# One core: v stores from the ScalarE queue to SP one unit later, z stores in half the issues, squares from GpSimd to ScalarE

## The chip, the cores and the metric

The kernel runs on one core of a Trainium2 chip. The metric is the device time of one execution in microseconds. Five engines work side by side, each with its own queue in order: TensorE (PE, with its weight loads PEld), VectorE (DVE), ScalarE (ACT), GpSimd (POOL) and SyncE (SP), which only issues DMAs. Time before the change: 1584.96 us, median of three runs (1580.27 to 1590.88).

## The reference

The input x has 8 batches of 3072 rows and 256 columns. Three things follow each other:

```
X = rfft(x, axis=1);  Y = soft(X @ (w_r + i w_i) + bias);  y = irfft(Y)        # soft: shrink by 0.01, real and imaginary
h = max(y @ w_in, 0);  g = (s * h^2 + b) @ w_out                               # 256 -> 2048 -> 256
logits = g @ w_gate;  e = argmax(logits)                                       # 8 experts
out[t] = p(t) * (max(g[t] @ w1[e], 0) @ w2[e])  for the first 768 tokens of each expert, 0 for the others
```

## The kernel before

The transform along 3072 = 48 x 64 rows is done as matrix products in stages, with the intermediate results in device memory. For a batch b: `f1_mm` (eight steps) multiplies x by the 48-point matrix, ScalarE copies the result to `z` and four DMAs store it to `zd`. Then twelve *groups* p: `g_load` loads a pair `zp`; `g_a` multiplies it by the second transform matrix (PE `pf`, L278; ScalarE copy `l`, L281); `g_b` and `g_b2` mix the channels with the weights (PE `pmx`, L355) and add the bias on VectorE (L364, L375 to L378); `g_soft` clips and subtracts on VectorE (`cl` L349, `t` L350); `g_c` multiplies by the inverse matrix (PE `pi`, L393), ScalarE copies to `v` (L395) and the ScalarE queue issues the store to `vd` (L397). Eight *inverse steps* follow: `i2_load` loads `u` from `vd` (L403), `i2_mm` multiplies it (PE `pi`, L419), ScalarE casts the result to `ah` (L422), GpSimd squares `ah` into `asq` (L425, bf16), and VectorE transposes the same PSUM tile into `at` (L434), which is stored to `ad` (L439).

The dense layer works on `ah` in *units*: `s_unit` has four products of 384 columns into one PSUM tile `ph` (L757), ScalarE's relu `r` (L762) and VectorE's square `qb` (L763). Eight units are one i, 64 units a batch, 512 units the kernel. A tile `ph`, the forward step's `pz` and the inverse step's `pi` share two PSUM buffers (tag `h`); the tile of an inverse step is free when both the cast and the transposes have read it. After eight units `lg_set` turns the squares and `asq` into logits (bounds that tell which tokens are certainly of one expert), `lg_out` copies them (L793) and `lg_fin` reduces them (L804). Tokens that the bounds leave open go into a list (GpSimd indirect DMAs, L911) and are computed exactly in the tail; batch 1 also holds four *exact blocks* (`x_steps`), whose squared rows `xq` are stored to `sd`.

The order of the work around the units is written by a planner in `run`: each unit k has a list of steps with ranks (loads 0, groups 1, second loads 2, logits 3, forward steps 4, inverse steps 5, zero stores of `out` 6, L1978). The groups of batch b + 1 run beside the units of batch b, from unit 64b - GROUP_LEAD on, a new group every five units, with the steps of a group 0, 2, 4, 4.1 and 8 units after its start; `g_load` is put six units ahead. Batch 1's groups have a schedule of their own (from unit 26, one every two units). The inverse steps and the forward steps of batch b + 2 are put where a cost is least: the load of a unit, 3 more if the unit already has such a step, 1 more for each neighbour that has one, and what the next unit lacks to 1.5. A step may put stores into the list `later`; they are issued in the next unit, right after `s_unit`, before that unit's other steps:

```
self.s_unit(b, i, u)
while self.later:
    self.later.pop(0)()
for e in sorted(plan.pop(64 * b + k, []), key=lambda e: e[:3]):
    e[3]()
```

Before the change the z and `at` stores go by `later` to SP; the v stores, the squares and the exact blocks' stores are issued at once.

Of the kernel before, what the change touches and what calls it, by code (L numbers as in the profile page):

```python
# [14 lines left out]
AF = mybir.ActivationFunctionType  # L15
ALU = mybir.AluOpType
# [3 lines left out]
C = 256  # L20
# [3 lines left out]
M1 = 48  # L24
# [7 lines left out]
TD = 256  # L32
# [92 lines left out]
S_FROM, S_TO = 19, 62  # L125
LIST_AT = 60
XP = 3
INV_LOAD_AT = 54
FIRST_GROUPS_AT = 26
GROUP_LEAD = 9  # L130
GROUP_CYCLE = 5
GROUP_STEPS = (("g_a", 0), ("g_b", 2), ("g_b2", 4), ("g_soft", 4.1), ("g_c", 8))
FIRST_STEPS = (("g_a", 0.3), ("g_b", 1.3), ("g_b2", 2), ("g_soft", 2.6), ("g_c", 5))
# [17 lines left out]
class Kern:  # L151
# [54 lines left out]
    def f1_load(self, b, c):  # L206

        xv = self.I["x"][b].rearrange("(a n) c -> a n c", n=M2)
        if b == 0 and c % 2 == 1:
            xs = [self.stage()[:, 0:2 * C].rearrange("p (n c) -> p n c", n=2) for k in range(2)]  # L210
            for k in range(2):
                for r in range(2):
                    n2 = 8 * c + 4 * r + 2 * k
                    self.nc.sync.dma_start(out=xs[k][64 * r:64 * r + M1], in_=xv[:, n2:n2 + 2, :])
        else:
            pool, tag = (self.mo, "u") if b == 0 and c > 3 else (self.wk, "x")
            xp = pool.tile([128, 4, C], F32, tag=tag, name="x", bufs=4 if tag == "x" else 3)
            for r in range(2):
                n2 = 8 * c + 4 * r
                self.nc.sync.dma_start(out=xp[64 * r:64 * r + M1], in_=xv[:, n2:n2 + 4, :])  # L220
            xs = [xp[:, 0:2], xp[:, 2:4]]
        self.xt[b, c] = xs

    def f1_mm(self, b, c):

        nc = self.nc
        xs = self.xt.pop((b, c))
        if b or c % 2 == 1:
            ph = self.hp.tile([128, 2, 512], F32, tag="h", name="pz")
            ps = [ph[:, 0], ph[:, 1]]  # L230
        else:
            ps = [self.psum("pz") for r in range(2)]
        for k in range(2):
            for r in range(2):
                h = slice(64 * r, 64 * r + M1)
                nc.tensor.matmul(ps[r][64 * k:64 * k + 64, :], self.f1[h], xs[k][h].rearrange("p a c -> p (a c)"),  # L236
                                 start=True, stop=True, skip_group_check=True)
        if b:
            zz = self.wk.tile([128, 2, 2, C], F32, tag="z", name="z", bufs=2)
            nc.scalar.copy(out=zz.rearrange("p r a c -> p r (a c)"), in_=ph)  # L240

            def store():
                for r in range(2):
                    for k in range(2):
                        n2 = 8 * c + 4 * r + 2 * k
                        nc.sync.dma_start(out=self.zs[b][n2:n2 + 2].rearrange("n q c -> q n c"), in_=zz[64 * k:64 * k + M1, r])
            self.later.append(store)
            return
        for r in range(2):
            t = 2 * c + r  # L250
            k = t % 11
            pool, tag, n = ((self.wk, "v", 3), (self.wk, "t", 3), (self.mo, "ah", 2), (self.mo, "asq", 2),
                            (self.wk, "zp", 3))[min(k // 2, 4)]
            z = pool.tile([128, 2, C], F32, tag=tag, name="z", bufs=n)
            if r == 1:
                nc.vector.tensor_copy(out=z.rearrange("p a c -> p (a c)"), in_=ps[r])
            else:
                nc.scalar.copy(out=z.rearrange("p a c -> p (a c)"), in_=ps[r])
            for k in range(2):
                n2 = 8 * c + 4 * r + 2 * k  # L260
                nc.sync.dma_start(out=self.zs[b][n2:n2 + 2].rearrange("n q c -> q n c"), in_=z[64 * k:64 * k + M1])
# [126 lines left out]
    def g_c(self, b, p):  # L388
        nc = self.nc
        t = self.Y.pop((b, p))  # L390
        ps = self.psum("pi1")
        for gi in range(2):
            nc.tensor.matmul(ps[:, gi * C:(gi + 1) * C], self.e[:, 2 * p + gi], t[:, gi * C:(gi + 1) * C], start=True, stop=True)  # L393
        v = self.wk.tile([128, 512], F32, tag="v", name="v", bufs=3)
        nc.scalar.copy(out=v, in_=ps)  # L395
        dst = self.vd[b].rearrange("n (r g) c -> (n r) (g c)", r=4)
        nc.scalar.dma_start(out=dst[:, 2 * p * C:(2 * p + 2) * C], in_=v)  # L397


    def i2_load(self, b, i):  # L400
# [6 lines left out]
    def i2_mm(self, b, i):  # L407

        nc = self.nc
        u = self.u.pop((b, i))  # L410
        ah = self.aT[b, i] = self.mo.tile([128, 2, TC], F32R, tag="ah", name="ah", bufs=2)
        ps = self.hp.tile([128, 2, 512], F32, tag="h", name="pi2")
        for h in range(2):
            for n in range(4):
                for r in range(2):
                    o = ps[:, r, 4 * M1 * h:4 * M1 * (h + 1)].rearrange("p (m n) -> p m n", n=4)
                    p = slice(64 * r, 64 * r + M1)
                    for k in range(2):
                        nc.tensor.matmul(o[64 * k:64 * k + 64, :, n], u[p, n, 128 * k + h:128 * k + 128:2], self.f1t[p],  # L419
                                         start=True, stop=True, skip_group_check=True)  # L420
        pv = ps[:, :, :TC].rearrange("p r (m n) -> p m r n", n=4)
        nc.scalar.copy(out=ah.rearrange("p h (m r n) -> p (h m) r n", r=2, n=4), in_=pv)  # L422
        af = ah.bitcast(F32)
        self.asq[b, i] = self.mo.tile([128, 2, TC], BF16, tag="asq", name="asq", bufs=2)
        nc.gpsimd.tensor_tensor(out=self.asq[b, i], in0=af, in1=af, op=ALU.mult)  # L425
        self.at[b, i] = pv

    def i2_rows(self, b, i):
# [21 lines left out]
    def f1_items(self, b):  # L450
        it = []
        for k in range(8):
            def f(k=k):
                self.f1_mm(b, k)
                if b:
                    self.x_ahead(8 * b + k + (XP if b < 3 else XP - 1))
            it.append(f)
        return it

    def x_ahead(self, n):  # L460

        while self.xn <= min(n, 8 * self.B - 1):
            self.f1_load(*divmod(self.xn, 8))
            self.xn += 1
# [535 lines left out]
    def x_steps(self, dtile, lgpool, ga, out, m0, hidden, rows, ptile, keep=None, yout=None):  # L1000

        nc = self.nc
# [7 lines left out]
                x["y"] = ptile("ya").rearrange("p (m c) -> p m c", m=2)  # L1010

        def mm(v):
            ps = hidden()
            self.x_mm(ps, x["a"], v)
            q = qs[v] = rows()
            nc.scalar.activation(out=q, in_=ps, func=AF.Relu)
            nc.vector.tensor_tensor(out=q, in0=q, in1=q, op=ALU.mult)
            if yout is not None:
                ys[v] = self.x_out(x["y"], q, v)
            if keep is not None:  # L1020
                nc.sync.dma_start(out=keep[2 * v:2 * v + 2, :, 128 * m0:128 * m0 + TD].rearrange("f p n -> p f n"), in_=q)

        def lg(v):
            for k in (v, v + 1):
# [434 lines left out]
    def rows(self, yr, ids):  # L1459
        self.gather(yr, self.yx, ids)  # L1460
# [302 lines left out]
    def run(self):  # L1763
        tc, nc, B = self.tc, self.nc, self.B
# [5 lines left out]
        with ExitStack() as es, tc.manual_schedule():  # L1770
# [97 lines left out]
            def put(at, f, rank=1):  # L1868
                e = plan.setdefault(int(at), [])
                e.append((rank, at, len(e), f))  # L1870
# [17 lines left out]
            def groups(b):  # L1888
                at, cyc, steps = 64 * (b - 1) - GROUP_LEAD, GROUP_CYCLE, GROUP_STEPS
                if b == 1:  # L1890
# [19 lines left out]
            def plan_batch(b):  # L1910
# [62 lines left out]
                if b + 1 < B:  # L1973
                    put(u + INV_LOAD_AT, lambda: (self.i2_load(b + 1, 0), self.i2_load(b + 1, 1)), 2)
                for z in range(len(ZERO_AT)):
# [20 lines left out]
            for b in range(B):  # L1996
                if b == B - 1:
                    e2.close()
                    p2 = es.enter_context(tc.tile_pool(name="p2", bufs=1, side="right", reuse_waits="tile"))
                    e4 = es.enter_context(ExitStack())  # L2000
                    self.p2c = e4.enter_context(tc.tile_pool(name="p2c", bufs=1, side="right", reuse_waits="tile"))
                    self.yf = [p2.tile([128, C], F32, tag=f"yf{j}", name=f"yf{j}") for j in range(NJ)]
                if b:
                    plan_batch(b)
                for k in range(64):
                    i, u = divmod(k, 8)
                    self.s_unit(b, i, u)
                    while self.later:
                        self.later.pop(0)()
                    for e in sorted(plan.pop(64 * b + k, []), key=lambda e: e[:3]):  # L2010
                        e[3]()
                    assert b < B - 1 or k < LIST_AT or not todo
                    if todo:
                        todo.pop(0)()
                    if u == 7:
                        del self.aT[b, i]
# [29 lines left out]
```

## Time and profile before

| | |
|---|---|
| median of three runs | 1584.96 us |
| the profiled execution | 1582.95 us, span 1580.9 us |
| mean granted clock of TensorE | 0.941 |
| busy: PE, DVE, ACT, POOL | 1402.5, 961.3, 800.7, 268.6 us |
| DMA queue 1 (SP) | 200.13 MB, 47.9% of the 16 engines' span |
| DMA queue 10 (ScalarE) | 25.20 MB, 4.4% |

Busy times are of the whole span, in which stages with different limits follow each other: constants, the first transform and the conversion of the weights up to about 127 us, the 512 units from there to about 1411 us, and the exact tail after that. By the start of their first unit the batches 0 to 7 begin at 126.8, 341.7, 545.0, 702.1, 845.4, 991.7, 1135.3 and 1263.5 us. A wait is put down to the operation whose end released it.

### The profile page before, as it was taken

The page shows a single profiled execution, that of the slowest core. Times are in us where ns is not written, and L with a number is a line of the kernel's source. Part 1 is how long each engine was busy: PE and PEld are TensorE (multiplying, and loading weights), DVE is VectorE, ACT ScalarE, POOL GpSimd, SP SyncE. Part 2 cuts the span into 40 slices and gives each one's busy share as a digit, 9 for nine tenths or more (in the row PEclk, how much of TensorE's full clock was granted, in tenths as well). Part 3 has the DMA queues.
Part 4 walks back from the last instruction along what each step waited for, and adds up shares of the span by engine and source line. Part 5 has one row for each costly group of instructions (what it writes and reads, how often), then busy time and mean ns, then how long its engine had stood idle before and what let it go on. Part 6 is the DMA issues. An engine that isn't in the chain of part 4 may idle for free. (4 is left out here: it accounts for less than half of the span.)

```text
span 1580.9 us, 32575 instructions
## 1 busy us (share of the span) xinstructions
PE 1402.5 (89%) x12797; PEld 1153.8 (73%) x12797; DVE 961.3 (61%) x2078; ACT 800.7 (51%) x1132; POOL 268.6 (17%) x235
## 2 busy tenths in 40 slices
PE   6995859989999988999999999999999868999984
PEld 3975637778788766777777877777888747988872
DVE  1775426765655877667677756776687675653410
ACT  1334533455555655665665655565656555652311
POOL 0444110000000013002010200110030171223020
PEclk8897879999999989999999989999999988999997
DMA  8726685645655545655755755565445456630052
GB/s 201 243 90 189 159 209 145 182 127 155 182 162 154 136 113 154 163 148 125 190 141 148 170 140 152 134 180 140 135 108 136 104 142 174 161 107 18 15 196 100
DMA packets 271370, 230.40 MB, mean 146 GB/s; under 512 B 123582, under 2 KB 231872, under 8 KB 271201
## 3 DMA queue, kind: packets, MB, share of 16 engines
q1 hardware_dynamic: 253408, 200.13, 47.9%
q10 hardware_dynamic: 13968, 25.20, 4.4%
q0 software_dynamic: 3824, 2.82, 0.7%
q8 instruction: 105, 1.72, 0.4%
q14 instruction: 65, 0.52, 0.1%
HBM read 114.17 MB, written 114.09 MB: 144 GB/s over the span
## 5 line engine op out<-in xcount | busy, mean ns | idle before, releaser
L762 ACT ACTIVATE r<-ph 128x768 bf16<-128x768 f32 (+1 forms) x512 | 399.6, 784 | 283.7 <-PE ph L757 250.6
L757 PE MATMUL ph<-ah,win 128*128 128x384 f32 (+1 forms) x2048 | 498.4, 369 | 36.4 <-ACT r L762 20.1
L763 DVE TENSOR_TENSOR qb<-r 128x768 bf16<-128x768 bf16 (+1 forms) x512 | 299.8, 587 | 269.3 <-ACT r L762 266.0
L757 PEld LDWEIGHTS ph<-ah,win 128*128 128x128 f32 x2048 | 350.8, 197 | 130.5 <-ACT r L762 54.2
L355 PE MATMUL pmx<-wm,l 128*128 128x256 f32 x1196 | 302.6, 392 | 8.0 <-DVE l L317 2.8
L425 POOL TENSOR_TENSOR asq<-ah 128x768 bf16<-128x768 f32 x64 | 95.9, 1498 | 969.3 <-ACT ah L422 953.7
L355 PEld LDWEIGHTS pmx<-wm,l 128*128 128x128 f32 x1196 | 229.7, 197 | 40.0 <-DVE l L317 3.6
L278 PE MATMUL pf<-d,zp 128*128 128x128 f32 x672 | 93.3, 283 | 23.8 <-DMA zp<-zd 23.8
L278 PEld LDWEIGHTS pf<-d,zp 128*128 128x128 f32 x672 | 89.2, 198 | 27.4 <-DMA zp<-zd 26.4
L393 PE MATMUL pi<-t,e 128*128 128x256 f32 x384 | 99.4, 382 | 1.0 <-DVE t L378 0.6
L236 PE MATMUL pz<-x,f 48*64 48x512 f32 x480 | 78.4, 697 | 14.6 <-DVE at L434 9.5
L419 PEld LDWEIGHTS pi<-f1t,u 48*64 48x64 f32 x4096 | 68.7, 136 | 29.1 <-issue 11.9
L419 PE MATMUL pi<-f1t,u 48*64 48x48 f32 x4096 | 76.7, 224 | 11.5 <-ACT z L240 6.8
L434 DVE STREAM_TRANSPOSE at<-pi 128x384 f32<-128x384 f32 x128 | 66.9, 560 | 26.9 <-ACT ah L422 22.3
L240 ACT COPY z<-pz 128x1024 f32<-128x1024 f32 x56 | 56.7, 1013 | 50.9 <-PE pz L236 30.5
L911 POOL DMA_INDIRECT list<-c,x x64 | 64.8, 1012 | 82.6 <-DVE c L907 66.7
L393 PEld LDWEIGHTS pi<-t,e 128*128 128x128 f32 x384 | 71.5, 191 | 7.6 <-PE ph L757 1.1
L350 DVE TENSOR_TENSOR t<-t,cl 128x512 f32<-128x512 f32 x96 | 74.6, 777 | 3.3
L422 ACT CAST ah<-pi 128x768 fp32r<-128x768 f32 x64 | 51.2, 801 | 49.1 <-PE pi L419 49.1
L395 ACT COPY v<-pi 128x512 f32<-128x512 f32 x96 | 56.3, 587 | 38.2 <-PE pi L393 33.2
L281 ACT COPY l<-pf 128x512 f32<-128x512 f32 x84 | 49.3, 587 | 51.6 <-PE pf L278 47.4
L793 ACT COPY ls<-lg 128x384 f32<-128x384 f32 (+1 forms) x64 | 53.6, 837 | 19.4 <-PE lg L780 15.2
(408 smaller groups left out, 1815.5 us busy)
## 6 DMA issues: line engine op xcount, KB each, us to landing
zd<-z SPq DMA_DIRECT2D x256, 96.0 KB
zp<-zd SPq DMA_DIRECT2D x96, 256.0 KB
vd<-v ACTq DMA_DIRECT2D x96, 256.0 KB
u<-vd SPq DMA_DIRECT2D x128, 192.0 KB
ad<-at SPq DMA_DIRECT2D x256, 96.0 KB
out<-zero SPq DMA_DIRECT2D x96, 256.0 KB
x<-x SPq DMA_DIRECT2D x120, 192.0 KB
sd<-xq SPq DMA_DIRECT2D x32, 256.0 KB
```

The lines of the kernel that those rows point to most:

```text
L236: nc.tensor.matmul(ps[r][64 * k:64 * k + 64, :], self.f1[h], xs[k][h].rearrange("p a c -> p (a c)"), start=True, stop=True, skip_group_che ...
L278: nc.tensor.matmul(pv[:, h, :, gi * 64:gi * 64 + 64], zp[:, gi, h * 128:(h + 1) * 128], self.d[:, 2 * p + gi, :].rearrange("p (t m) -> p t ...
L350: nc.vector.tensor_tensor(out=t, in0=t, in1=cl, op=ALU.subtract)
L355: self.nc.tensor.matmul(o, part(h), w[:, h], start=start and h == 0, stop=stop and h == 1, skip_group_check=True)
L393: nc.tensor.matmul(ps[:, gi * C:(gi + 1) * C], self.e[:, 2 * p + gi], t[:, gi * C:(gi + 1) * C], start=True, stop=True)
L419: nc.tensor.matmul(o[64 * k:64 * k + 64, :, n], u[p, n, 128 * k + h:128 * k + 128:2], self.f1t[p], start=True, stop=True, skip_group_check ...
L425: nc.gpsimd.tensor_tensor(out=self.asq[b, i], in0=af, in1=af, op=ALU.mult)
L434: nc.vector.transpose(out=at[:, :, :, h], in_=pv[:, M1 * h:M1 * (h + 1)])
L757: nc.tensor.matmul(ps[:, j, :n], self.win[:, k, f], ah[:, k, t0:], start=(k == 0), stop=(k == 1))
L762: nc.scalar.activation(out=r, in_=ps[:, :, :n], func=AF.Relu)
L763: nc.vector.tensor_tensor(out=q, in0=r, in1=r, op=ALU.mult)
L911: self.nc.gpsimd.indirect_dma_start(out=self.lists[n], out_offset=bass.IndirectOffsetOnAxis(ap=x[:, n:n + 1], axis=0), in_=c[:, n:n + 1], ...
```

## The change

The v stores of batches 1 to 7 go to SP through `later`, so one unit after the copy; batch 0's stay on the ScalarE queue. For batches 1 to 7 a forward step loads x so that the two z tiles of a step hold neighbouring rows, and z is stored by two DMAs of 192 KB in place of four of 96 KB. The squares `asq` are an activation on ScalarE, put into `later`, so they stand behind the relu of the next unit. The exact blocks' stores go into `later`, which is also emptied at the start of every `mm` of `x_steps`. GROUP_LEAD goes from 9 to 10 and INV_LOAD_AT from 54 to 55, so that the groups of batches 2 to 7 run one unit earlier and the first two u loads of the next batch one unit later.

```diff
-INV_LOAD_AT = 54
+INV_LOAD_AT = 55
-GROUP_LEAD = 9
+GROUP_LEAD = 10
@@ f1_load
-                n2 = 8 * c + 4 * r
-                self.nc.sync.dma_start(out=xp[64 * r:64 * r + M1], in_=xv[:, n2:n2 + 4, :])
+                n2 = 8 * c + (2 if b else 4) * r
+                src = xv[:, n2:n2 + 4, :] if not b else xv[:, 8 * c:8 * c + 8, :].rearrange("a (k r n) c -> a r k n c", k=2, r=2)[:, r]
+                self.nc.sync.dma_start(out=xp[64 * r:64 * r + M1] if not b else xp[64 * r:64 * r + M1].rearrange("p (k n) c -> p k n c", k=2), in_=src)
@@ f1_mm
-                for r in range(2):
-                    for k in range(2):
-                        n2 = 8 * c + 4 * r + 2 * k
-                        nc.sync.dma_start(out=self.zs[b][n2:n2 + 2].rearrange("n q c -> q n c"), in_=zz[64 * k:64 * k + M1, r])
+                for k in range(2):
+                    n2 = 8 * c + 4 * k
+                    nc.sync.dma_start(out=self.zs[b][n2:n2 + 4].rearrange("n q c -> q n c"),
+                                      in_=zz[64 * k:64 * k + M1].rearrange("p r a c -> p (r a) c"))
@@ g_c
-        nc.scalar.dma_start(out=dst[:, 2 * p * C:(2 * p + 2) * C], in_=v)
+        def store():
+            (nc.sync if b else nc.scalar).dma_start(out=dst[:, 2 * p * C:(2 * p + 2) * C], in_=v)
+        if b:
+            self.later.append(store)
+        else:
+            store()
@@ i2_mm
-        nc.gpsimd.tensor_tensor(out=self.asq[b, i], in0=af, in1=af, op=ALU.mult)
+        self.later.append(lambda q=self.asq[b, i]: nc.scalar.activation(out=q, in_=af, func=AF.Square))
@@ x_steps, mm
+            self.flush()
...
-                nc.sync.dma_start(out=keep[2 * v:2 * v + 2, :, 128 * m0:128 * m0 + TD].rearrange("f p n -> p f n"), in_=q)
+                self.later.append(lambda: nc.sync.dma_start(
+                    out=keep[2 * v:2 * v + 2, :, 128 * m0:128 * m0 + TD].rearrange("f p n -> p f n"), in_=q))
@@ run
-                    while self.later:
-                        self.later.pop(0)()
+                    self.flush()
```

`flush` is the loop that stood in `run`.

## Rows read from the trace of the kernel before

**Rows 1.** Busy time by stretch: PE, PEld, DVE, ACT, POOL, clock, DMA share, GB/s.
```profile
126.80:341.70 214.90, 173.25 (x1678) 135.94 (x1679) 122.25 (x282) 101.17 (x165) 35.90 (x34) 0.89 0.63 171
341.70:545.00 203.30, 195.86 (x1845) 161.83 (x1844) 126.61 (x277) 110.31 (x155) 11.88 (x8) 0.99 0.55 155
545.00:1263.50 718.50, 671.72 (x6411) 545.92 (x6410) 505.37 (x1077) 425.23 (x554) 106.30 (x88) 0.96 0.55 144
```

**Rows 2.** Waits of TensorE, 545 to 1263.5 us: total, times, longest.
```profile
PE pf L278 <- DMA zp<-zd: 15.3, 5, 6.9
PE ph L757 <- DVE at L434: 12.8, 7, 1.8
PE pz L236 <- DVE at L434: 9.5, 4, 4.1
PE ph L757 <- ACT r L762: 4.2, 9, 0.9
```

**Rows 3.** Waits of SP's queue, 545 to 1263.5 us.
```profile
SPq L1978 <- DMA vd<-v: 53.6, 11, 7.0
SPq L246 <- DMA vd<-v: 47.8, 12, 7.9
SPq L267 <- DMA vd<-v: 33.3, 5, 10.5
```

**Rows 4.** Timeline 763 to 776 us, one late zp load: start, us, instruction, idle before.
```profile
763.80 1.81 SPq L246 DMA_DIRECT2D zd<-z  x4
...
769.92 0.33 ACTq L397 DMA_DIRECT2D vd<-v  x1
...
771.99 0.36 SPq L267 DMA_DIRECT2D zp<-zd  x1
...
775.72 0.58 PE L278 MATMUL pf<-d,zp 128*128 128x128 f32 x1 [2.45 <-DMA zp<-zd]
```

**Rows 5.** Timeline 809 to 815 us, one late pair of transposes.
```profile
810.29 1.47 POOL L425 TENSOR_TENSOR asq<-ah 128x768 bf16<-128x768 f32 x1 [17.04 <-ACT ah L422]
810.55 1.48 DVE L349 TENSOR_SCALAR cl<-t 128x512 f32<-128x512 f32 x1
...
812.77 1.05 DVE L434 STREAM_TRANSPOSE at<-pi 128x384 f32<-128x384 f32 x2
...
813.88 0.97 PE L757 MATMUL ph<-ah,win 128*128 128x384 f32 x4 [1.83 <-DVE at L434]
```

**Rows 6.** The lines L349 and L425: durations in ns, minimum, median, maximum.
```profile
L349 DVE TENSOR_SCALAR cl<-t x96: 416/427/1492, 51.5 to 1245.2; 128x512 f32<-128x512 f32 x96
...
L425 POOL TENSOR_TENSOR asq<-ah x64: 1457/1467/1919, 126.8 to 1390.2; 128x768 bf16<-128x768 f32 x64
```

**Rows 7.** Busy time in four half-clock stretches behind zp waits (625.4, 775.6, 919, 1065.8).
```profile
sum 30.20, PE 23.85 PEld 16.62 DVE 10.98 ACT 8.42 POOL 4.59; mean PE 5.96 PEld 4.16 DVE 2.74 ACT 2.11 POOL 1.15
```

**Rows 8.** Six half-clock stretches behind at waits (564, 669.8, 721, 864.4, 1011.1, 1236.4).
```profile
669.80:673.10 3.30, 3.30 (x10) 2.85 (x10) 1.50 (x4) 0.81 (x1) 0.00 (x0) 0.50 0.57 138
...
sum 26.60, PE 22.75 PEld 17.37 DVE 18.55 ACT 9.28 POOL 0.00; mean PE 3.79 PEld 2.89 DVE 3.09 ACT 1.55 POOL 0.00
```

**Rows 9.** Waits of TensorE, 126.8 to 341.7 us.
```profile
PE pf L278 <- DMA zp<-zd: 8.5, 2, 7.1
PE pi L419 <- ACT z L240: 6.8, 1, 6.8
```

**Rows 10.** ScalarE groups by line: busy us, mean ns, idle before.
```profile
L395 ACT COPY v<-pi 128x512 f32<-128x512 f32 x96 | 56.3, 587 | 38.2 <-PE pi L393 33.2 <-DMA zd<-z 1.1
L422 ACT CAST ah<-pi 128x768 fp32r<-128x768 f32 x64 | 51.2, 801 | 49.1 <-PE pi L419 49.1
...
L980 ACT CAST eh<-xq 128x512 fp32r<-128x512 f32 x16 | 9.9, 619 | 15.1 <-DVE xq L1017 9.4 <-PE ya L989 5.7
```

**Rows 11.** ScalarE groups by line: table loads after the start (L1075 likewise).
```profile
L727 ACT ACT_TABLE_LOAD x2 | 2.6, 1283 | 0.0
```

**Rows 12.** Waits of TensorE, 1263.5 to 1411 us.
```profile
PE pbc L1208 <- POOL bc L1199: 7.2, 1, 7.2
```

More of the change, by code (lines that the diff above doesn't have):

```diff
@@ L458, in f1_items, with flush @@
         return it
+    def flush(self):
+        while self.later:
+            self.later.pop(0)()
     def x_ahead(self, n):
```

## The prediction

> **What bounds the kernel now.** I read the busy time by stretch first, because the kernel has stages with different limits [rows 1]. From 545 to 1263.5 us five of the eight batches run, 5 x 64 = 320 units, so a unit lasts 2.25 us. TensorE is busy for 671.7 of these 718.5 us, VectorE for 505.4, ScalarE for 425.2, GpSimd for 106.3. TensorE bounds this stretch; 46.8 us of it is TensorE idle, and more is lost where its clock is halved. So I asked what ends TensorE's waits there [rows 2]: 15.3 us are five waits for a `zp` load (the z pair that `g_a` multiplies), 12.8 + 9.5 us are eleven waits for the transposes `at` on VectorE, and only 4.2 us are waits for ScalarE's relu. Two causes hold 37.6 of 46.8 us, and the change touches both.
>
> **Why a zp load is late.** SP's own waits show it [rows 3]. In this stretch the zero stores of `out` waited 53.6 us for a landing of `vd<-v`, the z stores 47.8, the zp loads 33.3. None of the three reads or writes `vd`: this is not their data. SP's queue is held by the completion of a v store that ScalarE issues, and that ScalarE issues only when it comes to it. In [rows 4] SP issues four z stores at 763.80, then nothing; ScalarE issues the v store at 769.92; SP's next issue, a zp load, comes at 771.99, the time at which that store has landed; TensorE stands still for 2.45 us until 775.72. The zp load was planned six units ahead of its `g_a`, and the wait ate that lead.
>
> **Why `at` is late.** One of the ten waits of about 1.82 us ((22.3 - 4.1) / 10 [rows 2]) is in [rows 5]. GpSimd squares `ah` from 810.29 on; VectorE's clip, started at 810.55, takes 1.48 us, where its median over 96 is 0.427 [rows 6]. Behind it in the same queue stand a subtraction and the two transposes that free the PSUM buffer TensorE needs next. Without the square beside it the clip would end 1.05 us sooner, and so would TensorE's wait.
>
> **What a wait costs beyond itself.** Behind these waits the granted clock is 0.50, that is the lower of the two levels, 1.2 GHz. The stretches at 0.50 behind the zp waits hold 23.85 us of TensorE work [rows 7], those behind five of the ten 1.82 us waits and the 4.1 us one 22.75 us [rows 8]. At the full level this would take half: 11.9 and 11.4 us are lost, at most.
>
> **The change, part by part.**
> *v stores to SP, one unit later (84 of 96; batch 0's stay).* In SP's own order a z, zero or zp issue can no longer stand behind a store that another engine has not yet issued. What SP now waits for is ScalarE's copy of v, which by the time of the flush is one unit old. Queued behind that wait are the unit's loads: zp (six units ahead of use), u (eight), x (two or three forward steps); a unit of delay fits into each. Gain: between 0 and 15.3 us [rows 2]. I take the whole but half of the longest wait (6.9), which lies among the list's indirect stores: 15.3 - 3.4 = 11.9 us. ScalarE also loses 84 issues of 0.33 us [rows 4]; it is not the bound, so nothing. For VectorE and TensorE nothing moves.
> *z in two issues in place of four.* 112 issues fewer, of 1.81 / 4 = 0.45 us each [rows 4], 51 us of SP's queue, against 84 x 0.33 = 28 us added. Bytes and row sizes of z stay. The x loads for b > 0 now read 2 KB pieces where they read 4 KB; DMA is busy for 0.55 of the stretch [rows 1] and the loads are far ahead: nothing. Only in batch 0 is SP's queue near the path: from 126.8 to 341.7 us TensorE waits 8.5 us for zp and 6.8 us for a z copy held back by a z store [rows 9]. Between 0 and 15.3; I take a third, 5 us, since half the issues go but the loads between them stay.
> *Squares to ScalarE.* GpSimd loses 64 x 1.467 us; the lock-out of VectorE goes. I went through the planner's cost rule with the groups one unit earlier: before, the inverse step falls into a unit with `g_b2` and `g_soft` at units 5, 30, 45 of a batch, afterwards at 14 and 29. Two a batch over five batches are ten again, each 1.05 us shorter: 10.5 us (between 0 and the 18.2 that they hold now). About 0.8 us of each wait stays: the four sums, the clip and the subtraction still stand ahead of `at`.
> Price of a square on ScalarE: no row has it. A cast of 512 columns from SBUF takes 0.619 us, and 768 columns cost 0.801 - 0.587 = 0.214 us more than 512 from PSUM [rows 10]: 0.83 us, 64 of them 53 us. It is covered by ScalarE's own slack: 425.2 + 40 x 0.83 = 458 of 718.5 us. In the unit after an inverse step ScalarE has a relu of the cast's shape, 0.80, a square, 0.83, and one copy, 0.59 [rows 10], 2.2 us of work, against a unit of 2.25, with two PSUM buffers between. I take 0 and keep 53 as the other end. The kernel loads a ScalarE table four times after its start, 1.283 us each [rows 11]; were squares not in one of these sets, up to four loads, 5 us, would be added. I take 0.
> *Exact blocks' stores put off, groups and inverse loads shifted.* In batch 1, which holds those blocks, TensorE is busy for 195.9 of 203.3 us [rows 1]; there is nothing to win or to hide behind: 0, within the 7.4 us of idle either way. The last v store of a batch is flushed in unit 54 and the u load comes in 55, used in unit 60: five units, 11 us; I take 0. Were it a unit late in each of seven batches, 16 us would be lost.
> *Last batch.* TensorE's 7.2 us wait there is for a chain on GpSimd [rows 12] with a square in front of it; one square less (1.5 us) is a gain, eight squares beside a busy ScalarE a loss: 0, from -6 to +2.
> *Clock.* Of 11.9 + 11.4 us I take half, 11.7: a wait of 0.8 us stays, and waits that the change does not touch stay too.
>
> Sum: 11.9 + 10.5 + 5 + 11.7 = 39.1 us. The profiled execution took 1582.95 us, 2.0 under the median of 1584.96; from the median this gives 1546 us. What is late next is TensorE itself, with ScalarE second.
>
> **A rule against it.** SP is held by ScalarE's stores [rows 3, 4]. The Trainium skill (DMA: Bandwidth & Descriptors, section Issuing engines are not separate DMA queues) says that transfers issued from different engines interleave on the same DMA engines, and that issuing from several engines saves only the issuing time. By it the moved stores would save nothing but 84 issues, which is rival 1 below. The rows say otherwise, since SP sat idle, not the DMA engines.
>
> **The rivals.**
> 1. *The store's issuer does not matter*: zp stays late, for the loads queue behind the same landings. For: the longest wait lies among indirect stores. Against: [rows 4]. The zp term and its clock go, and batch 0's 5 us, which are of the same kind; 10.5 us and half of 11.4 remain, 16.2: 1569 us. Chance 0.14.
> 2. *Loads stuck behind the v store on SP*: SP waits in order for ScalarE's copy, and each batch keeps its zp wait (11.9 + 6 us not won) and gets another of 15.3 / 5 = 3.1 us with its half clock: about 20 us more. For: SP already waits for VectorE and for landings through the stretch. Against: six units are 13 us of lead. 39 - 18 - 20 = 1: 1584 us. Chance 0.10.
> 3. *Squares on the path, slower*: a relu that stands behind a square ends too late for TensorE, which has two PSUM buffers to write on; this decides once ScalarE falls a unit, 2.25 us, behind. Price 53 us against 39 won: 1599 us. For: batches 0 and 7 have more ScalarE work. Against: TensorE waits for relu for only 4.2 us now [rows 2]. Chance 0.09.
> 4. *The forecast*, 1525 to 1565, most likely 1546: chance 0.60. The last 0.07 are mixtures.
>
> **The numbers.** Faster or slower counts from 1%, 16 us, which is about what a measurement of this kernel can tell from no change. Range: below, all terms at their upper ends, 15.3 + 18.2 + 15.3 + 23.3 = 72, would give 1513; with some of it kept, 1522. Above it takes in rival 1 and rival 2: 1584. Faster: 0.58 of the forecast, half of rival 1, 0.05 of the mixtures: 0.70. Same: the rest of rival 1, most of rival 2 and some mixtures: 0.19. Slower: 0.11.
>
> **What would show it.** In the profile after: no SP wait for `vd<-v` but the u loads'; no TensorE wait for zp in the five batches; VectorE's clip with a maximum near 0.43 us; ten waits for `at` of about 0.8 us; fewer stretches at 0.50 of the clock between 545 and 1230 us; TensorE's wait for relu still under 10 us in the five batches; a square of about 0.83 us. It would be wrong if TensorE's waits for zp moved to other places, or if relu rows showed idle TensorE in the unit after each square.

## The result and the profile after

The changed kernel takes 1521.98 us (median of four, 1519.61 to 1525.56) where the kernel before takes 1584.39: a ratio of 0.960 (0.957 to 0.964), 62 us won where 39 were forecast. It lies 0.02 us below the range, which began at 1522. The profiled execution took 1525.56 us, span 1523.8, against 1582.95 and 1580.9: 57 us between the two profiles, and these I account for.

By the start of first and last units the span falls into stages:

| stage | before, us | after, us | difference |
|---|---|---|---|
| up to the first unit | 126.8 | 127.6 | +0.8 |
| batch 0 | 214.9 | 211.7 | -3.2 |
| batch 1 | 203.3 | 201.7 | -1.6 |
| batches 2 to 6 | 718.5 | 668.8 | -49.7 |
| batch 7, to its last unit | 144.6 | 138.4 | -6.2 |
| last unit and tail | 172.8 | 175.6 | +2.8 |

Busy time by stretch after the change, columns as in [rows 1]: batch 0, batch 1, batches 2 to 6, and the part of these that runs without a break of the clock.

```profile
127.60:339.30 211.70, 175.58 (x1683) 137.62 (x1683) 119.49 (x282) 107.23 (x175) 23.12 (x25) 0.87 0.64 174
339.30:541.00 201.70, 194.99 (x1847) 160.96 (x1845) 123.94 (x277) 115.87 (x163) 0.00 (x0) 1.00 0.55 156
541.00:1209.80 668.80, 650.08 (x6407) 534.40 (x6406) 473.35 (x1075) 450.53 (x592) 45.88 (x48) 0.99 0.61 154
565.00:1203.00 638.00, 624.29 (x6166) 512.75 (x6169) 450.43 (x1000) 434.02 (x569) 45.88 (x48) 1.00 0.61 156
```

In the third line TensorE does the same products (6407 records against 6411 in [rows 1]) in 650.1 us in place of 671.7. The granted clock stays at 1.00 from 565 to 1203 us. The stretches at 0.50 in batches 2 to 6, eleven before and two after, sum to:

```profile
sum 61.30, PE 50.09 PEld 37.15 DVE 32.34 ACT 19.20 POOL 5.88; mean PE 4.55 PEld 3.38 DVE 2.94 ACT 1.75 POOL 0.53
```

```profile
sum 13.30, PE 11.15 PEld 9.71 DVE 7.84 ACT 5.16 POOL 0.00; mean PE 5.57 PEld 4.85 DVE 3.92 ACT 2.58 POOL 0.00
```

At the full level this work takes half, so (50.09 - 11.15) / 2 = 19.5 of the 21.6 us are the clock; the other 2.1 are not settled. TensorE's idle time is 18.7 us where it was 46.8: 28.1 us. With the 21.6 these make the 49.7.

TensorE's waits in batches 2 to 6 (total, times, longest):

```profile
PE pz L237 <- DVE at L441: 5.4, 7, 0.8
PE pnr L735 <- DVE nrm L728: 4.1, 1, 4.1
PE ph L768 <- ACT r L773: 3.0, 8, 0.9
...
PE ph L768 <- DVE at L441: 1.5, 2, 0.8
```

Against [rows 2], the zp waits are gone, the `at` waits are nine of 0.77 us, and the relu waits are no longer than before. The wait of 4.1 us for `nrm`, a chain on VectorE early in batch 2, was 1.2 us before: there the `at` wait of 4.1 us [rows 2] followed it within 2 us. So of that `at` wait little is won. SP's own waits there, to be set against [rows 3]:

```profile
SPq L400 <- ACT v L396: 122.7, 35, 7.1
...
SPq L410 <- DMA vd<-v: 8.2, 5, 2.1
```

SP now waits for the copy of v, and only the u loads wait for a landing of v. VectorE's clip from the first unit on, and the square (ns, minimum, median, maximum), as in [rows 6]:

```profile
L350 DVE TENSOR_SCALAR cl<-t x84: 416/427/474, 242.9 to 1189.2; 128x512 f32<-128x512 f32 x84
```

```profile
L432 ACT ACTIVATE asq<-ah x64: 833/836/862, 128.8 to 1331.0; 128x768 bf16<-128x768 f32 x64
```

The clip's maximum falls from 1492 to 474 ns (the twelve clips ahead of the first unit go up to 928 ns in both kernels, beside other work of GpSimd), and a square costs 836 ns where 0.83 us was estimated. In batch 7 the wait of [rows 12] halves:

```profile
PE pbc L1221 <- POOL bc L1212: 3.5, 1, 3.5
```

### The profile page after: what moved, and what is told of

The parts are those of the page before. It is cut to its first block, busy times and chain, and to the rows that moved or that the text cites. A ratio compares the mean times of both kernels' runs of the same rounds, so it can differ in the third digit from the quotient of the medians.

```text
span 1523.8 us, 32398 instructions
## 1 busy us (share of the span) xinstructions
PE 1383.0 (91%) x12797; PEld 1145.2 (75%) x12797; DVE 920.3 (60%) x2078; ACT 843.0 (55%) x1196; POOL 170.9 (11%) x171
## 4 chain that ended last, share of the span: by engine, by line
PE 68%; DVE 13%; DMA 6%; ACT 5%; issue 4%; SPq 2%; POOL 1%; another core or an unknown queue 0%; POOLq 0%; DVEq 0%; ACTq 0%
PE ph L768 19%; PE pmx L356 15%; PE pz L237 4%; PE pi L394 4%; PE pf L279 3%; PE pi L426 3%; ACT r L773 3%; PE phx L985 3%; PE ya L1449 3%; PE lg L788 2%; DVE qb L774 2%; PE ph L985 2%; PE ya L1000 1%; PE ph L1496 1%; PE plt L812 1%
## 5 line engine op out<-in xcount | busy, mean ns | idle before, releaser
L768 PE MATMUL ph<-ah,win 128*128 128x384 f32 (+1 forms) x2048 | 490.1, 365 | 20.9 <-ACT r L773 14.5
L774 DVE TENSOR_TENSOR qb<-r 128x768 bf16<-128x768 bf16 (+1 forms) x512 | 274.9, 539 | 267.8 <-ACT r L773 263.5
L768 PEld LDWEIGHTS ph<-ah,win 128*128 128x128 f32 x2048 | 346.7, 195 | 109.4 <-ACT r L773 44.8
L356 PE MATMUL pmx<-wm,l 128*128 128x256 f32 x1196 | 296.0, 386 | 5.9 <-DVE l L318 2.9
L356 PEld LDWEIGHTS pmx<-wm,l 128*128 128x128 f32 x1196 | 225.3, 193 | 34.1 <-DVE l L318 3.7
L279 PE MATMUL pf<-d,zp 128*128 128x128 f32 x672 | 89.7, 277 | 7.0 <-DMA zp<-zd 6.0
L237 PE MATMUL pz<-x,f 48*64 48x512 f32 x480 | 73.4, 655 | 11.3 <-DVE at L441 6.1
L429 ACT CAST ah<-pi 128x768 fp32r<-128x768 f32 x64 | 51.3, 801 | 46.8 <-PE pi L426 43.3
L1029 DVE TENSOR_TENSOR xq<-xq 128x512 f32<-128x512 f32 x48 | 33.1, 691 | 46.6 <-ACT xq L1028 46.5
```

What stands on the lines that cost most here:

```text
L279: nc.tensor.matmul(pv[:, h, :, gi * 64:gi * 64 + 64], zp[:, gi, h * 128:(h + 1) * 128], self.d[:, 2 * p + gi, :].rearrange("p (t m) -> p t ...
L356: self.nc.tensor.matmul(o, part(h), w[:, h], start=start and h == 0, stop=stop and h == 1, skip_group_check=True)
L768: nc.tensor.matmul(ps[:, j, :n], self.win[:, k, f], ah[:, k, t0:], start=(k == 0), stop=(k == 1))
L774: nc.vector.tensor_tensor(out=q, in0=r, in1=r, op=ALU.mult)
```

## The experiments

Times are medians, ratios are to the kernel before on the same chip, with 95% intervals. The runs lie on different chips, on which the kernel before took from 1582 to 1599 us, so ratios are compared across chips and microseconds only within one. Stretches of batches 2 to 6 are read from first unit to first unit of each trace.

**One part at a time.** Theory: v's move to SP takes the zp waits and their clock, the squares' move takes the lock-out of VectorE, and the two add. Rival: the issuer of v does not matter.

*e1_pool_squares.*

```diff
-        self.later.append(lambda q=self.asq[b, i]: nc.scalar.activation(out=q, in_=af, func=AF.Square))
+        nc.gpsimd.tensor_tensor(out=self.asq[b, i], in0=af, in1=af, op=ALU.mult)
```

> The changed kernel with one part undone: the squares are again on GpSimd, at once. Theory (two separate causes, each with its half-clock stretches): the VectorE lock-out comes back, ten waits for the transposes of about 1.8 us in the five batches, half of them followed by the clock at 0.50, and the GpSimd chain of the last batch is late again; no wait for a zp load in the five batches. About 1522 + 10.5 + 10 + 5 = 1547 us. Rival (the squares hold nearly all of the gain): 1575 to 1585 us. Rival (the stores hold nearly all): 1522 to 1530 us.

1553.74 us, 0.978 (0.973 to 0.982): the `at` waits are back with 18.2 us in ten, no zp wait.

```profile
PE pz L237 <- DVE at L441: 14.5, 8, 1.8
...
PE ph L768 <- DVE at L441: 3.7, 2, 1.8
```

Six of the ten are followed by a stretch at 0.50. Beside the v part the squares are worth 0.017 of the time, 27 us.

*e2_only_squares.* The kernel before with the one line:

```diff
-        nc.gpsimd.tensor_tensor(out=self.asq[b, i], in0=af, in1=af, op=ALU.mult)
+        self.later.append(lambda q=self.asq[b, i]: nc.scalar.activation(out=q, in_=af, func=AF.Square))
```

> The kernel before with one part done: the squares on ScalarE, behind the relu of the next unit; all else as before. Theory: the waits for the transposes fall to 0.8 us each, the waits for zp stay with their half-clock stretches, 1584 - 25 = about 1560 us. Rival (squares lie on ScalarE's path): 1584 to 1620 us. Rival (squares hold nearly all of the gain): 1525 to 1535 us.

A miss: 1597.82 us, 1.004 (1.001 to 1.007), no gain at all, although the `at` waits fell. The time lies in the range of the rival that puts the squares on ScalarE's path; whether that is the reason, e11 and e9 below answer. TensorE's waits in batches 2 to 6 show what took it:

```profile
PE pi L419 <- issue: 25.5, 41, 1.1
PE pf L278 <- DMA zp<-zd: 8.1, 5, 3.7
PE pz L236 <- DVE at L434: 6.4, 4, 4.1
PE ph L757 <- DVE at L434: 5.6, 7, 1.0
```

The first line is new: TensorE stands still inside the 64 small products of an inverse step, waiting for nothing that the profile shows. One such place in the timeline (start, us, instruction, idle before):

```profile
880.45 0.69 PE L419 MATMUL pi<-f1t,u 48*64 48x48 f32 x28
881.02 1.07 POOL L911 DMA_INDIRECT list<-c,x  x1 [0.30 <-issue]
...
884.38 0.28 PE L419 MATMUL pi<-f1t,u 48*64 48x48 f32 x3 [1.08 <-issue]
...
885.80 0.37 PE L419 MATMUL pi<-f1t,u 48*64 48x48 f32 x4 [1.14 <-issue]
...
889.57 0.80 ACT L422 CAST ah<-pi 128x768 fp32r<-128x768 f32 x1 [5.79 <-PE pi L419]
```

This is the stretch in which GpSimd issues the eight list stores of a batch, 1.2 us apart. While GpSimd did the squares, a square in its queue split such a row: five of the six rows in batches 2 to 6 last 13.4 to 14.3 us in the kernel before. In e2 all six last 9.7 to 10.1 us.

*e3_v_act_now* and *e4_v_act_late.* The changed kernel with v on the ScalarE queue, at once or put off (the last five lines of the cut are e3's alone):

```diff
-            (nc.sync if b else nc.scalar).dma_start(out=dst[:, 2 * p * C:(2 * p + 2) * C], in_=v)
+            nc.scalar.dma_start(out=dst[:, 2 * p * C:(2 * p + 2) * C], in_=v)
-        if b:
-            self.later.append(store)
-        else:
-            store()
+        store()          # e3 only
```

> The changed kernel with one part undone: the v stores of all batches are issued by ScalarE right behind the copy. Theory: SP again waits for landings of v in front of loads that do not read it, zp waits come back in some batches with half-clock stretches, 1522 + 15 to 30 = about 1545 us. Rival (the issuer does not matter): 1520 to 1526 us.

> The changed kernel with the v stores put off by one unit as there, but on the ScalarE queue. It parts the issuer from the moment. Theory (SP is held by a store that another engine has not yet issued): as with the stores at once on ScalarE or worse, 1540 to 1560 us, with SP waiting for v's landing before zp and zero issues. Rival (only the putting off counts): 1520 to 1526 us.

1581.75 us, 0.993 (0.991 to 0.996), and 1567.78 us, 0.986 (0.982 to 0.990). Both are slower than theory and rival had it. So the queue matters, but not by way of zp: neither has a zp wait of note in batches 2 to 6. e3 loses 9 us in batch 1 (211.1 us against 201.7); much of the rest of both lies in the stretches of the list stores again. From the first store of a row to 3 us behind its last, summed over the eight rows, TensorE is idle for 30.8 us in e3, 30.5 in e4 and 8.9 in the changed kernel. In e4:

```profile
862.35 0.37 ACTq L400 DMA_DIRECT2D vd<-v  x1
862.39 7.88 SPq L246 DMA_DIRECT2D zd<-z  x2
862.67 0.92 POOL L922 DMA_INDIRECT list<-c,x  x1 [129.35 <-DVE c L918]
...
865.99 0.33 PE L791 MATMUL lg<-asq,bed 128*32 128x384 bf16 x2
...
871.57 0.92 POOL L922 DMA_INDIRECT list<-c,x  x1 [0.30 <-issue]
...
874.14 0.81 ACT L804 COPY ls<-lg 128x384 f32<-128x384 f32 x1 [7.89 <-remote]
...
875.00 0.64 PE L812 MATMUL plt<-ident,ls 128*96 128x128 f32 x4 [4.50 <-ACT ls L804]
```

The row of 7.88 us merges two z stores of SP. Each issue lasts 0.33 us (ns, minimum, median, maximum, first and last start):

```profile
L246 SPq DMA_DIRECT2D zd<-z x2: 327/328/328, 862.4 to 869.9; - x2
```

In the 7.2 us between them SP stands still: the second z store carries the same completion semaphore in the trace (103, a counter that a transfer raises when it has landed) as the v store that ScalarE issued at 862.35, and waits for it. The ScalarE copy `ls`, whose product ended at 866.3 (the line of L791), starts only at 874.14, after the last list store; TensorE waits 4.50 us for it.

**The list stores.** New theory: eight list stores in a row hold back the other engines, unless something spaces them. The test holds them one unit apart, in all batches but the last, with a 0.2 us GpSimd copy of one column of the unit's `qb` ahead of each:

```diff
-        self.q[b, i, u] = q
+        self.q[b, i, u] = self.mark = q
...
-    def to_list(self, n, x, c):
+    def to_list(self, n, x, c, paced=False):
+        if paced:
+            tick = self.rt("tick", [1], BF16)
+            self.nc.gpsimd.tensor_copy(out=tick, in_=self.mark[:, 0, 0:1])
```

It went onto the kernel before (e15), e2 (e11), e4 (e12), e3 (e14) and the changed kernel (e13).

> The kernel before with the squares on ScalarE (1598 when run alone, with 23.2 us of TensorE waits inside the inverse transform's matmuls, all while the eight list stores of a batch run) and the list stores held one unit apart by a small GpSimd copy that reads that unit's q. Theory (the eight list stores in a row hold back everything else): those 23 us go below 6 and some 10 us of half clock with them, 1560 to 1570. Rival (ScalarE's added work makes the waits, the list stores only run at the same time): the waits stay, 1595 to 1600.

> The changed kernel with the v stores, put off, on ScalarE's queue (1568 when run alone) and the list stores held one unit apart in the same way. Theory (what the SP queue gives v is only that the list stores no longer stall TensorE): the 21 us of waits in front of plt and inside pi go, and half of the 18 us at half clock in those stretches: 1530 to 1542. Rival (ScalarE's queue costs by itself, at every v store): 1560 to 1570.

> The kernel before with the list stores held one unit apart, nothing else. Theory (there GpSimd's squares already spread them): 1580 to 1590 beside 1587. Rival (the pacing is itself a gain, whatever the change): 1555 to 1565.

> The changed kernel with the v stores issued by ScalarE at once, as before (1582 when run alone), and the list stores held one unit apart. Theory (putting off the v store is worth little, the list stores made the rest): 1522 to 1535. Rival (a v store issued at once costs ScalarE's queue at every unit, as the 11 us between this and the put-off one with list stores in a row suggest): 1535 to 1550.

> The changed kernel with the list stores held one unit apart. Theory (its own list stores hold TensorE back by little: 9.7 us of waits in those stretches, 5.4 of them at POOL's bc in the last batch): 1515 to 1522 beside 1522 for the changed kernel. Rival (the pause of the transfers that the list stores bring is still paid elsewhere): 1500 to 1510.

| kernel | list stores in a row | held apart |
|---|---|---|
| before | 1 | 0.992 (0.988 to 0.996), e15 |
| before, squares on ScalarE | 1.004 (1.001 to 1.007), e2 | 0.978 (0.973 to 0.982), e11 |
| after, v at once on ScalarE | 0.993 (0.991 to 0.996), e3 | 0.972 (0.965 to 0.978), e14 |
| after, v put off on ScalarE | 0.986 (0.982 to 0.990), e4 | 0.959 (0.955 to 0.962), e12 |
| after | 0.960 (0.957 to 0.964) | 0.965 (0.959 to 0.971), e13 |

The theory held for e11 and e12 (1553.30 and 1521.49 us, both better than its numbers). e11 differs from e2 by the spacing alone, and its first waits in batches 2 to 6 show no `issue` line:

```profile
PE pf L278 <- DMA zp<-zd: 15.3, 6, 7.0
PE pz L236 <- DVE at L434: 6.4, 4, 4.1
```

e12 is the sharpest: one small copy per list store makes the ScalarE queue as good for v as SP's. e13 (1534.86 us) and e14 (1544.40) missed, where the kernel before took 1593.89: the spacing brings the changed kernel nothing that can be measured, and a v store issued at once costs 0.013 more than one put off on the same queue (e12, on another chip), as e14's rival had it. Against e13, on the same chip with v put off on SP's queue, it costs 9.5 us, 0.006. On the kernel before, e15 gains a little, 1579.84 us, against its theory and far from its rival. e12 around the same place as e4 above:

```profile
841.34 0.35 ACTq L400 DMA_DIRECT2D vd<-v  x1
841.39 7.59 SPq L246 DMA_DIRECT2D zd<-z  x2
...
843.58 0.94 POOL L925 DMA_INDIRECT list<-c,x  x1 [0.58 <-issue]
845.36 0.89 ACT L804 COPY ls<-lg 128x384 f32<-128x384 f32 x1
846.23 0.19 POOL L924 COPY tick<-qb 128x1 bf16<-128x1 bf16 x1 [1.71 <-DVE qb L774]
847.00 0.94 POOL L925 DMA_INDIRECT list<-c,x  x1 [0.58 <-issue]
```

Between its two z stores SP still waits for the landing of the v store:

```profile
SPq L246 <- DMA vd<-v: 6.9, 1, 6.9
```

So the pacing does not free SP; but the copy `ls` and TensorE go on. Over 14 us around it TensorE is busy 13.28 us in e12 and 9.50 in e4 (columns as in [rows 1]):

```profile
844.00:858.00 14.00, 13.28 (x146) 10.31 (x145) 10.79 (x23) 9.19 (x13) 7.30 (x13) 1.00 0.56 139
```

```profile
862.00:876.00 14.00, 9.50 (x65) 7.75 (x64) 5.40 (x13) 5.16 (x8) 7.69 (x8) 0.99 0.64 151
```

**What takes the zp waits away.** e6 is the kernel before with the two planner constants, e7 that with v put off to SP as well; e16 has constants, squares on ScalarE, spaced list stores and v put off on the ScalarE queue, e19 the same with v at once.

```diff
-INV_LOAD_AT = 54
+INV_LOAD_AT = 55
-GROUP_LEAD = 9
+GROUP_LEAD = 10
```

> The kernel before with only the two planner constants of the change (the groups' first step 10 units before a batch ends in place of 9, the inverse step's loads at 55 in place of 54). Theory (the stores' queue and the squares make the gain): the zp waits, the at waits and the spells of half clock behind them stay, 1585 to 1592 beside 1591. Rival (the plan alone moves the zp loads away from the stores that delay them): the 15.3 us of zp waits and some 12 us of clock behind them go, about 1564.

> The kernel before with the shift and the v stores of batch 1 on moved to SP one unit later; z in four issues, squares on GpSimd, exact blocks as before. Theory (v is what counts of the moved transfers, z and x nothing): near the changed kernel with the squares back on GpSimd, 1554, no zp waits in batches 2 to 6. Rival (the halved z issues on SP make the room for v): SP's longer queue makes loads late again, 1575 or more with zp waits of over 8 us.

> The kernel before with the squares on ScalarE, the two planner constants, the v stores put off by a unit but on ScalarE's queue, and the list stores held one unit apart; z in four issues, x loads and exact blocks as before. Theory (z, x and exact blocks are worth nothing, the order of stores and loads all): 1520 to 1528, zp waits under 5 us. Rival (the halved z issues take the zp waits away): near the squares with paced list stores alone, 1545 to 1553, zp waits of 12 us or more.

> The kernel before with the squares on ScalarE, the list stores held one unit apart and the two planner constants; the v stores at once on ScalarE's queue, z in four issues. Theory A (putting the v store off a unit takes the zp waits away): zp waits of 10 us or more in batches 2 to 6, 1545 to 1553 by a kernel before of 1587. Theory B (the shift of the groups does it, once the list stores are spaced): zp waits under 4 us, 1525 to 1540.

e6: 1579.03 us, 0.996 (0.993 to 0.999), zp waits 12.0 us; the constants alone hardly count: by the profiles they win 8 us in batches 2 to 6 and lose 10 in batch 1. Batch 1 is 211.1 to 213.7 us long in e3, e6, e14 and e19, the four with the shifted groups and v at once, and 200.0 to 205.1 in all other runs. e7: 1554.20, 0.978 (0.974 to 0.983), as e1, and no zp wait. e19: 1574.31, 0.984 (0.980 to 0.989), slower than either of its theories; e16: 1542.52, 0.971 (0.965 to 0.978), over its forecast by the ratio too (1520 to 1528 beside 1587 is 0.958 to 0.963), so that what it lacks against e12, the z issues, x loads and exact stores, may be worth some 0.012. The zp waits in batches 2 to 6, e19 first, then e16:

```profile
PE pf L278 <- DMA zp<-zd: 11.4, 4, 3.9
```

```profile
PE pf L278 <- DMA zp<-zd: 0.6, 1, 0.6
```

So putting the store off takes them away. But SP is held in e16 as it was before, by its own waits in that stretch:

```profile
SPq L445 <- DMA vd<-v: 66.3, 10, 11.6
SPq L246 <- DMA vd<-v: 35.9, 6, 7.6
...
SPq L267 <- DMA vd<-v: 28.4, 7, 5.9
```

And e14 has v at once on ScalarE's queue, and no zp wait either; against e19 it has z in two issues, the x loads in the new order and the exact blocks' stores put off. Either the putting off or these three together suffice.

**The smaller parts, beside a fresh run of the changed kernel on the same chip.** e5 has z in four issues and the x loads of before; e9 writes each square twice, the same values; e10 plans the inverse step ahead of the unit's group steps:

```diff
-        put(n, lambda i=i: self.i2_do(*divmod(8 * b + i + 1, 8)), 5)
+        put(n, lambda i=i: self.i2_do(*divmod(8 * b + i + 1, 8)), 0.5)
```

> The changed kernel once more, as the mark for the three others on the same chip: 0.958 to 0.965 of the kernel before. No theory differs here.

> The changed kernel with z stored in four issues and the x loads' order as before. Theory (SP has room for the issues, nothing waits for a z store): within 5 us of the changed kernel. Rival (the two issues less per z store make part of the gain that the other runs leave over): 10 to 20 us slower, with waits for zp or for the inverse loads' u.

> The changed kernel with every square on ScalarE done twice over (the second writes the same values), 64 more instructions of 0.84 us. Theory (they lie in ScalarE's idle time): 0 to 10 us slower. Rival (they are on the path by way of r, which ScalarE issues behind them): 35 to 55 us slower, with waits for r grown from 3.4 us to over 20.

> The changed kernel with the inverse step planned ahead of the other steps of its unit in place of behind them, so that VectorE does its transpose before the group's sums. Theory (the at waits left, 6.9 us in nine of about 0.77, come from the sums in front of the transpose): they go, 5 to 8 us faster than the changed kernel. Rival (the sums are then late themselves, or the inverse matmuls wait for their u): no gain or up to 10 us slower.

The mark is 1520.48 us, 0.961 (0.957 to 0.964). e5: 1527.82, 0.964 (0.961 to 0.967), 7 us slower by the medians with intervals that overlap, between its theory and its rival; its profile has 5.4 us of them in batch 0 (214.6 against 209.2). e9: 1525.84, 0.965 (0.961 to 0.968): 64 x 0.84 = 54 us more ScalarE work cost some 5 us, with intervals that overlap. Its waits for relu in batches 2 to 6:

```profile
PE ph L769 <- ACT r L774: 8.0, 13, 1.1
```

e10: 1510.08 us, 0.953 (0.949 to 0.956), 10 us better than the mark and outside its interval: the fastest version here. Its waits in batches 2 to 6:

```profile
PE pmx L356 <- DVE l L283: 2.6, 3, 1.1
...
PE ph L768 <- DVE at L441: 0.8, 1, 0.8
```

Eight of nine `at` waits are gone (6.1 us), for 2.6 us of waits for the group's sums (0.6 in the mark). Of the 8.1 us between the two profiles 4.5 lie in batches 2 to 6 and 4.4 in batch 7, where the cause was not looked for.

## Why the prediction fell short, point by point

- **Clock: the step that failed.** "Of 11.9 + 11.4 us I take half, 11.7: a wait of 0.8 us stays." The sums above give 19.5 us. Nine of the ten stretches of [rows 7, 8] are gone; the one at 564 us stays, at 558 us, behind the wait for `nrm`. The nine waits of 0.77 us that stay do not bring the clock to its lower level: all nine lie in the unbroken stretch. It shows with one part changed as well: six of e1's ten waits of 1.6 to 1.8 us are followed by a stretch at 0.50, none of e11's ten of 0.8 to 1.0 us. In e10, where eight of the nine are gone, TensorE's busy time in batches 2 to 6 is that of the mark (649.9 and 649.7 us). The prediction had rows for waits of 1.8 us and more only [rows 8] and let the waits of 0.8 keep half of the loss. This is 7.8 of the missing 18 us between the profiles.
- **zp: right in size, the cause only in part.** 15.3 us went where 11.9 were forecast. The forecast said that SP was held by ScalarE's stores, and it was [rows 3, 4]. How, the records of the trace show: the v store at 769.92 and the zp load at 771.99 carry the same completion semaphore, 103, and SP waits for it. Of SP's waits of over 1 us in batches 2 to 6 of the kernel before, 203.7 us in 40 stand ahead of an issue whose semaphore was last used by a v store of ScalarE. But e16 and e14 keep SP held for over 100 us and have 0.6 us of zp waits and none. What counts is that the v store is put off, or that z goes in two issues together with the x loads and exact stores of the change. The longest wait, among the list stores, went as well (3.4 us).
- **`at`: mechanism right, 15.4 us for 10.5.** Ten waits of 1.82 became nine of 0.77 (11.3 us), as forecast: e1 brings back ten of 1.8 us. The working named three units of a batch (5, 30 and 45) and counted two; the trace before has ten waits in five batches, at about units 7 and 50 of batches 3 to 5. Not forecast: the one of 4.1 us, which is there in e2 and e11 and not in e6, and so went with the earlier groups. Most of it moved: the wait for `nrm` beside it grew by 2.9 us, to 5.7 us in e6.
- **Squares at nothing: right in the changed kernel**, where e9 doubles them for some 5 us; rival 3 had 53 for them. But the term was summed as if it stood alone, and alone it brings nothing (e2): the cost was not ScalarE's time but GpSimd's empty queue, which let the list stores run in a row. None of the rivals had this.
- **Rival 1, the issuer does not matter.** With the list stores apart its mechanism holds, at the price of the changed kernel: 0.959 on ScalarE's queue, 0.960 on SP's. The Trainium skill (DMA: Bandwidth & Descriptors, section Issuing engines are not separate DMA queues) says that transfers from different engines share the same DMA engines; e12 agrees, with 0.959 beside 0.960. With the list stores in a row it fails, 0.986 against 0.960, by waits of TensorE and ScalarE and not by loads that come late.
- **Rival 2** did not come: SP waits 122.7 us for the copies of v, and no zp wait follows.
- **Batch 0 and the z issues.** 5 us forecast; batch 0 is 3.2 us shorter, and e5 gives 5.4 back in it. Over all traces batch 0 lasts 208.2 to 213.0 us with z in two issues and 210.3 to 215.9 with four.
- **Batch 7.** 0 forecast, 6.2 measured. The wait for `bc` is 3.7 us shorter and the relu waits 5.4 (13.7 to 8.3 us). The squares' leaving GpSimd is not shown to be the reason: e1, with the squares back there, has 1.0 us of the wait for `bc` and 138.7 us for the batch, e11, without them, 5.6 us of it. It stays open.

By profiles: 21.6 (19.5 of it the clock) + 15.3 + 15.4 in batches 2 to 6, less 2.6 for other waits that grew, `nrm` above all, 3.2 + 1.6 + 6.2 in the others, less 3.6 ahead and in the tail: 57.1 us. The medians add 5 us, since the profile of before was 1.4 under the median of its four runs, 1584.39, and that of after 3.6 over.

Open: what holds ScalarE's copy and TensorE's small products while list stores run in a row. The profile names no releaser ("issue", "remote"), and the spacing removes the wait without ending SP's wait for the v store. The spacing also moves the later list stores of a row beside other steps; no run parts the two. And a row alone need not cost: the one unsplit row of batches 2 to 6 in the kernel before (587.8 to 597.6 us) holds no idle TensorE.

## What to carry to other kernels

Before work is taken off an idle engine, look at what else its queue issues: that work may have been what kept its transfers apart, and then the part that loses alone wins with the other. When waits of a kind shrink under a microsecond, look at whether the clock still falls behind them before counting it as half lost; here it did not behind single waits of 0.8 us. Behind several close together it did: three of about 0.4 us within 2 us in e13, in three batches, and waits of 0.7 and 0.8 us, 2 us apart, in e10. That a queue is held is not yet the reason why a load is late: keep the holding and take the lateness away, as in e16, before naming the cause. And where an issue waits for a landing that is not its data, see whether the two carry the same semaphore.

## What the runs showed of the hardware

- Around a row of eight indirect stores of GpSimd, 1.2 us apart, TensorE was idle for 3.3 to 4.9 us (first store to 3 us behind the last, the six rows of batches 2 to 6) when ScalarE issued the v stores put off (e4), for 0 to 1.0 us when SP did (changed kernel), and for 0.7 to 1.5 us when the stores were spaced (e12).
- An issue on SP waited for a transfer of another engine that had used its semaphore last: in e4 the second of two z stores came 7.2 us after the first had been issued, in e12 6.9 us.
- From the first unit on, 13 clips of 128 x 512 fp32 on VectorE took 1.48 to 1.49 us beside a square on GpSimd, where the median is 0.427 (kernel before).
- A square of 128 x 768 fp32 from SBUF took 836 ns on ScalarE, 1467 on GpSimd [rows 6].
